# Transposing by DMA instead of by TensorE in an attention kernel followed by a feed-forward: q, k, tails and attention outputs

## Chip, cores, metric

The kernel runs on one core of a Trainium2 chip. The metric is the device time of one execution in microseconds. Before the change it was 450.04 us (median of 4 runs, 449.12 to 450.78). "Span" is the time of the profiled execution as its trace shows it, a little below the device time.

## The reference

Eight batches of eight heads of attention over 576 positions (head size 64) with a relative-position bias, then a bilinear feed-forward:

```python
scores = q @ k.T / 8 + bias[bucket(|i - j|), head]        # 8 x 8 x 576 x 576
attn   = exp(scores - max) / sum(...)
x      = (attn @ v) laid out as 4608 tokens x 512
out    = ((x @ w_a) * (x @ w_b)) @ w_out                   # w_a, w_b: 512 x 1536, w_out: 1536 x 512
```

## The kernel before

Work goes by pairs of heads: 32 pairs, four to a batch. 512 of the 576 positions are the main part; the other 64 are the tail. Pair `p` is worked on in step `p`. From step 4 on, each step also holds feed-forward units of four matmuls each (seven or eight in steps 4 to 8, nine in later ones), of a chunk of 512 tokens; chunk `c` is batch `c`'s main part and from chunk 1 on its units fill steps `4c+5` to `4c+8`. The kernel's matmuls take q and k with the head dimension on the partitions, and the attention output likewise, so all of them are transposed on TensorE into PSUM and copied to SBUF:

```python
def transposes(ps, src, p, tag):
    b, hp = divmod(p, 4)
    for t in range(NM):                                   # NM = 4 blocks of 128 x 128
        x = (st[p][tag][:, t, :, :] if early(b) else      # early: batches 0 and 1
             src[b % 2][:, 512 * t + 128 * hp:512 * t + 128 * hp + 128])
        nc.tensor.transpose(ps[:, 128 * t:128 * t + 128], x, ident[:, :])

def t_q(p, eng=None):
    ps = ps_tr.tile([128, 1024], BF16, tag="tr", name=f"trq{p}")
    transposes(ps, qn, p, "qr")
    nc.tensor.transpose(ps[:, SM:SM + 128], qkt[b % 2][:, 2 * hp:2 * hp + 2, :], ident[:, :])
    ...                                                   # one large copy and four of 64 x 64

def t_x(p, eng=None):                                     # attention output of pair p
    ps = ps_tr.tile([128, 1024], BF16, tag="tr", name=f"trx{p}")
    for jq in range(5):
        nc.tensor.transpose(ps[:, 128 * jq:128 * jq + 128], XG[p % 2][:, jq, :, :], ident[:, :])
    copy(eng, xn_sb[hp][:, SM * b:SM * b + SM], ps[:, 0:SM])
    copy(eng, xn_sb[hp][:, SM * B + ST * b:SM * B + ST * b + ST], ps[:, SM:S])

# one step s (cut, the lambdas left out): U is a place for feed-forward units
steps += [qk(s, 0), U, ex(s, 1), A(0, 1, 2), U, mul(s, 0), t_q(s + 1), U, mul(s, 1), qk(s, 2), ..., U,
          ex(s, 3), t_k(s + 1), U, mul(s, 2), A(3, 4), U, mul(s, 3), qk_tail(s), U, t_x(s - 1), U,
          mul_tail(s), U]
b = s // 4 + 1
if s > 4 and s % 4 == 1 and b < B:                        # loads of the next batch, on GpSimd's queue
    load_q(b, 0, 8); load_k(b, 0, 8); load_tails(b); load_v(b, 0, 8); load_vt(b)
```

A load stands in the program at some step, but in the traces below it starts when GpSimd has come to it, behind the loads before it, and the buffer that it overwrites has been read for the last time (a semaphore tells GpSimd so: at 207.26 us the q load goes out after 18.47 us of waiting for PE's `trq_3162`).

The softmax here doesn't subtract the row's maximum and nothing guards it: scores larger than these inputs give would overflow.

Of the kernel before, what the change touches and what calls it, by code (L numbers as in the profile page):

```python
# [13 lines left out]
def kernel(  # L14
# [11 lines left out]
    nc = tc.nc  # L26
    FP32 = mybir.dt.float32
    BF16 = mybir.dt.bfloat16
# [3 lines left out]
    B, H, S, Dh = 8, 8, 576, 64  # L32
    NB = 32
    NM = 4
    SM = 128 * NM
    ST = S - SM
# [6 lines left out]
    NP = B * H // 2  # L43
# [33 lines left out]
    ident = const.tile([128, 128], BF16, name="ident")  # L77
# [11 lines left out]
    qn = [wpool.tile([128, H * NM * Dh], BF16, name=f"qn{i}") for i in range(2)]  # L89
    kn = [wpool.tile([128, H * NM * Dh], BF16, name=f"kn{i}") for i in range(2)]  # L90
    vn = [wpool.tile([128, H * NM * Dh], BF16, name=f"vn{i}") for i in range(2)]
    qkt = [wpool.tile([128, H, Dh], BF16, name=f"qkt{i}") for i in range(2)]
    vm = [wpool.tile([128, H, NM, Dh + 1], BF16, name=f"vm{i}") for i in range(2)]
    vt = [wpool.tile([128, H // 2, 2, Dh + 1], BF16, name=f"vt{i}") for i in range(2)]

    QT = [wpool.tile([128, S + 2 * ST], BF16, name=f"QT{i}") for i in range(3)]
    KT = [wpool.tile([128, SM + 2 * ST], BF16, name=f"KT{i}") for i in range(3)]
    XG = [wpool.tile([128, 5, 2, Dh], BF16, name=f"XG{i}") for i in range(2)]

    NW = 3  # L100
# [9 lines left out]
    def early(b):  # L110
        return b < 2
# [24 lines left out]
    def load_v(b, h0, h1):  # L136
        load4(v, vn[b % 2], b, h0, h1)

    def load_tails(b):
        for src, o in ((q, 0), (k, 64)):  # L140
            nc.gpsimd.dma_start(out=qkt[b % 2][o:o + 64, :, :],
                                in_=src[b, :, SM:S, :].transpose([1, 0, 2]))

    def load_vt(b):
        for hh in range(2):
            nc.gpsimd.dma_start(  # L146
                out=vt[b % 2][64 * hh:64 * hh + 64, :, hh, 0:Dh],
                in_=v[b, hh:H:2, SM:S, :].transpose([1, 0, 2]))
# [15 lines left out]
    nc.sync.dma_start(out=oh_sb[0:NB, :], in_=oh_handle.ap())  # L164
    nc.scalar.dma_start(out=ident[:, :], in_=id_handle.ap())
    nc.vector.memset(zero_sb[:, :], 0.0)
    for i in range(2):
        nc.vector.memset(vt[i][0:64, :, 1, :], 0.0)
        nc.vector.memset(vt[i][64:128, :, 0, :], 0.0)
        nc.vector.memset(vt[i][0:64, :, 0, Dh:Dh + 1], 1.0)  # L170
        nc.vector.memset(vt[i][64:128, :, 1, Dh:Dh + 1], 1.0)
# [48 lines left out]
    for hp in range(H // 2):  # L220
# [3 lines left out]
        if hp == 0:  # L224
            for hh in range(2):
                nc.sync.dma_start(out=Wt_sb[64 * hh:64 * hh + 64, :, :],
                                  in_=bass.AP(tensor=tab, offset=hh * TB + 512,
                                              ap=[[1, 64], [2 * TB, H // 2], [1, 192]]))
    for i in range(3):
        nc.vector.memset(QT[i][0:64, S + ST:], 0.0)  # L230
        nc.vector.memset(QT[i][64:128, S:S + ST], 0.0)
        nc.vector.memset(KT[i][0:64, SM + ST:], 0.0)
        nc.vector.memset(KT[i][64:128, SM:SM + ST], 0.0)


    st = [dict() for _ in range(NP)]
# [1 line left out]
    def copy(eng, out, in_):  # L238
        if eng is nc.scalar:
            nc.scalar.activation(out=out, in_=in_, func=ACTF.Copy)  # L240
        else:
            nc.vector.tensor_copy(out=out, in_=in_)
# [11 lines left out]
                    "p (h t d) -> p t h d", h=2, t=NM))  # L254
            st[p][tag] = r

    def transposes(ps, src, p, tag):
        b, hp = divmod(p, 4)
        for t in range(NM):
            x = (st[p][tag][:, t, :, :] if early(b) else  # L260
                 src[b % 2][:, 512 * t + 128 * hp:512 * t + 128 * hp + 128])
            nc.tensor.transpose(ps[:, 128 * t:128 * t + 128], x, ident[:, :])

    def t_q(p, eng=None):
        b, hp = divmod(p, 4)
        ps = ps_tr.tile([128, 1024], BF16, tag="tr", name=f"trq{p}")
        transposes(ps, qn, p, "qr")
        nc.tensor.transpose(ps[:, SM:SM + 128], qkt[b % 2][:, 2 * hp:2 * hp + 2, :], ident[:, :])  # L268
        qT, kT = QT[p % 3], KT[p % 3]
        if early(b):  # L270
            copy(eng, qT[:, 0:SM].rearrange("d (p t) -> d p t", t=NM),
                 ps[:, 0:SM].rearrange("d (t p) -> d p t", t=NM))
            copy(eng, qT[:, SM:S], ps[:, SM:S])
        else:
            copy(eng, qT[:, 0:S], ps[:, 0:S])
        for hh in range(2):
            r = slice(64 * hh, 64 * hh + 64)
            nc.vector.tensor_copy(out=kT[r, SM + ST * hh:SM + ST * hh + ST], in_=ps[r, S:S + ST])
            nc.vector.tensor_copy(out=qT[r, S + ST * hh:S + ST * hh + ST], in_=ps[r, SM:S])

    def t_k(p, eng=None, pool=None, tag="tr"):
        b, hp = divmod(p, 4)
        ps = (pool or ps_tr).tile([128, 1024], BF16, tag=tag, name=f"trk{p}")
        transposes(ps, kn, p, "kr")
        copy(eng, KT[p % 3][:, 0:SM], ps[:, 0:SM])
        st[p]["at"] = [None] * NM

    def v_in(b, h0, h1):
        if b < 2:
# [4 lines left out]


    def qk(p, t0):
        qT, kT = QT[p % 3], KT[p % 3]
        for t in (t0, t0 + 1):
            ps = ps_sc.tile([128, 2, 512], FP32, tag="sc", name=f"qk{p}_{t}")
            for hh in range(2):  # L300
                r = slice(64 * hh, 64 * hh + 64)
                nc.tensor.matmul(out=ps[:, hh, :], lhsT=kT[r, 128 * t:128 * t + 128],  # L302
                                 rhs=qT[r, 0:SM], start=True, stop=True)
            st[p]["ps", t] = ps

    def ex(p, t):
# [9 lines left out]


    def qk_tail(p):
        hp = p % 4
        qT, kT = QT[p % 3], KT[p % 3]  # L320
        ps = ps_sc.tile([128, 2, 512], FP32, tag="sc", name=f"qkt{p}")
        for t in range(NM):
            nc.tensor.matmul(
                out=ps[:, 0, :].rearrange("p (h t c) -> p h t c", h=2, t=NM)[:, :, t, :],
                lhsT=kT[:, 128 * t:128 * t + 128], rhs=qT[:, S:S + 2 * ST],
                start=True, stop=True)
        nc.tensor.matmul(out=ps[:, 1, :], lhsT=kT[:, SM:SM + 2 * ST], rhs=qT[:, 0:SM],
                         start=True, stop=True)
        pt = ps_tr.tile([128, 512], FP32, tag="tr", name=f"qktt{p}")
        nc.tensor.matmul(out=pt[:, 0:ST], lhsT=kT[:, SM:SM + 2 * ST], rhs=qT[:, SM:S],  # L330
                         start=True, stop=True)
        st[p]["ps"] = (ps, pt)

    def ex_tail(p):
# [55 lines left out]

    def t_x(p, eng=None):
        b, hp = divmod(p, 4)
        ps = ps_tr.tile([128, 1024], BF16, tag="tr", name=f"trx{p}")
        for jq in range(5):
            nc.tensor.transpose(ps[:, 128 * jq:128 * jq + 128], XG[p % 2][:, jq, :, :], ident[:, :])  # L395
        copy(eng, xn_sb[hp][:, SM * b:SM * b + SM], ps[:, 0:SM])
        copy(eng, xn_sb[hp][:, SM * B + ST * b:SM * B + ST * b + ST], ps[:, SM:S])
        st[p].clear()
# [97 lines left out]
    for s in range(4, NP + 1):  # L496
        new = s < NP
        U = "unit"
        A = lambda *jq: (lambda: [av(s - 1, j) for j in jq])
        steps = []  # L500
        if new:
            steps += [lambda: (qk(s, 0), ex(s, 0))]
        if s == 4:
            steps += [A(0, 1, 2), lambda: ex(s, 1), lambda: t_q(s + 1), A(3, 4),
                      lambda: mul(s, 0), lambda: t_x(s - 1), U, lambda: mul(s, 1), U,
                      lambda: (qk(s, 2), ex(s, 2)), U, lambda: ex(s, 3), lambda: t_k(s + 1), U,
                      lambda: mul(s, 2), U, lambda: mul(s, 3), lambda: (qk_tail(s), ex_tail(s)),
                      U, U, lambda: mul_tail(s)]
        elif new:
            steps += [U, lambda: ex(s, 1), A(0, 1, 2), U, lambda: mul(s, 0)]  # L510
            if s + 1 < NP:
                steps += [lambda: t_q(s + 1)]
            steps += [U, lambda: mul(s, 1), lambda: (qk(s, 2), ex(s, 2)), U, lambda: ex(s, 3)]
            if s + 1 < NP:
                steps += [lambda: t_k(s + 1)]
            steps += [U, lambda: mul(s, 2), A(3, 4), U, lambda: mul(s, 3),
                      lambda: (qk_tail(s), ex_tail(s)), U, lambda: t_x(s - 1), U,
                      lambda: mul_tail(s), U]
        else:
            steps += [A(0, 1, 2), U, U, U, A(3, 4), U, U, U, lambda: t_x(s - 1), U, U, U]  # L520
        reorder(s + 1)
        b = s // 4 + 1
        if s > 4 and s % 4 == 1 and b < B:
            load_q(b, 0, 8)
            load_k(b, 0, 8)
            load_tails(b)
            load_v(b, 0, 8)
            load_vt(b)
        quota = quotas.get(s, 9)
        seen, put = 0, 0  # L530
        nu = sum(1 for x in steps if x is U)
        for x in steps:
            if x is U:
                seen += 1
                n = (quota * seen + nu - 1) // nu - put
                put_units(n)
                put += n
            else:
                x()
        if new:  # L540
            v_next(s)
# [31 lines left out]
```

## Time and profile before

| | before |
|---|---|
| device time | 450.04 us |
| span | 449.3 us |
| TensorE (PE) busy | 424.7 us, 95% |
| VectorE busy | 287.4 us, 64% |
| one steady step | 11.88 us |

From the profile's page: the span, the busy time of each engine, PE's busy tenths and granted clock (tenths of full speed) in 40 equal slices, and the chain of waits by engine.

```profile
span 449.3 us, 9012 instructions
PE 424.7 (95%) x3578; PEld 221.1 (49%) x3643; DVE 287.4 (64%) x838; ACT 245.8 (55%) x350; POOL 88.9 (20%) x117
PE   5676999999999999999999999999999999999995
PEclk8579999999999999999999999999999999999999
PE 83%; DVE 10%; DMA 3%; issue 2%; ACT 1%; SPq 0%; DVEq 0%; ACTq 0%
```

After the first four slices PE is never short of work and the clock is full: from 47 to 445 us PE is busy for 394.1 of 398.0 us at a granted clock of 1.00. What PE does is what the kernel costs. The timeline of PE in one step (start, duration, line, output<-input, count) shows what a transpose costs there:

```profile
189.54 0.44 PE L395 MATMUL trx_2895<-ident,XG_112 128*128 128x128 bf16 x5
189.82 0.38 PE L426 MATMUL po_3_2890<-wo,g_128 128*128 128x512 bf16 x1
...
192.84 0.38 PE L406 MATMUL pa_0_2939<-xn_123,wa_113 128*128 128x512 bf16 x1
```

The durations overlap: 128x512 matmuls are listed with 0.38 us each and start 0.21 to 0.22 us apart (188.68, 188.89, 189.11 us). The cost is the distance between starts: five transposes take 0.28 us, from 189.54 to 189.82. At 192.84 the fourth matmul of a new chunk reads `xn_123`, the output of the batch's last pair.

GpSimd's timeline at the same place, with the wait that ended before each issue in brackets:

```profile
187.55 1.23 POOL L146 DMA_DIRECT2D vt_104<-in_v_dram  x2 [17.29 <-PE av_3_2848 L376]
207.26 3.53 POOL L123 DMA_DIRECT2D qn_93<-in_q_dram  x4 [18.47 <-PE trq_3162 L268]
```

The q loads wait until PE has transposed the last of the old q, so they start at 207 us.

### The profile page before, as it was taken

How to read it: one execution, taken by the hardware profiler on the slowest of the kernel's cores; microseconds unless marked ns; L12 is line 12 of the kernel's file. 1: busy time of each engine (PE TensorE's matmuls, PEld its weight loads, DVE VectorE, ACT ScalarE, POOL GpSimd, SP SyncE). 2: the span in 40 equal slices, each digit the busy share in tenths (PEclk: the TensorE clock that was granted, in tenths of full speed). 3: DMA queues.
4: the chain of work that ended last, by engine and by line, in shares of the span. 5: the costliest groups of instructions: out<-in, count | busy, mean ns of one | idle time of the engine just before them, and what ended most of it. 6: DMA issues, size and time to landing. Idle time of an engine off the chain costs nothing.

```text
span 449.3 us, 9012 instructions
## 1 busy us (share of the span) xinstructions
PE 424.7 (95%) x3578; PEld 221.1 (49%) x3643; DVE 287.4 (64%) x838; ACT 245.8 (55%) x350; POOL 88.9 (20%) x117
## 2 busy tenths in 40 slices
PE   5676999999999999999999999999999999999995
PEld 2264455555555555555555555555555554444442
DVE  5579789668766787577856786587658862330320
ACT  2678566556655665566556665566556652322321
POOL 9456365010801070105200350100000000000000
PEclk8579999999999999999999999999999999999999
DMA  9999999420942097207912290200010002002004
GB/s 101 219 200 203 192 148 76 82 65 1 107 72 63 15 84 72 77 25 49 104 49 54 16 137 27 76 1 1 23 71 2 1 1 94 1 0 93 1 1 94
DMA packets 87370, 30.35 MB, mean 68 GB/s; under 512 B 64760, under 2 KB 82712, under 8 KB 87328
## 3 DMA queue, kind: packets, MB, share of 16 engines
q0 software_dynamic: 80144, 18.88, 45.0%
q1 hardware_dynamic: 6992, 10.86, 7.3%
q8 instruction: 28, 0.46, 0.4%
q14 instruction: 14, 0.11, 0.1%
q10 hardware_dynamic: 192, 0.03, 0.0%
HBM read 39.18 MB, written 9.45 MB: 108 GB/s over the span
## 4 chain that ended last, share of the span: by engine, by line
PE 83%; DVE 10%; DMA 3%; issue 2%; ACT 1%; SPq 0%; DVEq 0%; ACTq 0%
DMA Wt<-bias_tab 2%; DVE XG_111 L387 1%; DVE g_125 L419 1%; DVE g_124 L419 1%; PE warm L208 1%; PE po_1_1335 L426 1%; PE po_0_1275 L426 1%; DMA bias_tab<-tab_sb 1%; PE po_1_2057 L426 1%; PE po_1_4869 L426 1%; PE po_1_3463 L426 1%; PE po_1_2760 L426 1%; PE po_1_4166 L426 1%; PE po_2_1403 L426 1%; PE po_3_6071 L426 1%
## 5 line engine op out<-in xcount | busy, mean ns | idle before, releaser
L416 PEld LDWEIGHTS <-wb_118 128*128 128x128 bf16 x144 | 12.4, 97 | 16.6 <-issue 5.6
L406 PEld LDWEIGHTS <-wa_114 128*128 128x128 bf16 x144 | 12.5, 98 | 15.3 <-issue 3.4
L416 PEld LDWEIGHTS <-wb_117 128*128 128x128 bf16 x144 | 12.4, 97 | 14.9 <-issue 4.7
L406 PEld LDWEIGHTS <-wa_113 128*128 128x128 bf16 x144 | 12.5, 98 | 14.6 <-issue 3.0
L416 PEld LDWEIGHTS <-wb_116 128*128 128x128 bf16 x144 | 12.3, 97 | 14.9 <-issue 5.1
L406 PEld LDWEIGHTS <-wa_115 128*128 128x128 bf16 x144 | 12.7, 98 | 13.4 <-issue 2.5
L123 POOL DMA_DIRECT2D qn_93<-in_q_dram x12 | 11.0, 925 | 38.6 <-PE trq_3162 L268 18.5
L123 POOL DMA_DIRECT2D qn_94<-in_q_dram x12 | 10.6, 886 | 40.2 <-PE trq_2459 L268 18.5
L146 POOL DMA_DIRECT2D vt_104<-in_v_dram x8 | 4.9, 620 | 53.7 <-PE av_3_2848 L376 17.3
L132 POOL DMA_DIRECT2D kn_95<-in_k_dram x12 | 10.6, 906 | 6.8 <-DVE qr_844 L251 6.6
L146 POOL DMA_DIRECT2D vt_103<-in_v_dram x8 | 5.0, 640 | 34.8 <-PE av_3_2145 L376 17.3
L132 POOL DMA_DIRECT2D kn_96<-in_k_dram x12 | 10.6, 912 | 0.0
L395 PEld LDWEIGHTS <-XG_112 128*128 128x128 bf16 x80 | 5.8, 98 | 5.4 <-DVE XG_112 L387 1.5
L395 PEld LDWEIGHTS <-XG_111 128*128 128x128 bf16 x80 | 5.8, 98 | 5.1 <-DVE XG_111 L387 1.8
L302 PEld LDWEIGHTS <-KT_108 64*128 64x128 bf16 x88 | 2.8, 95 | 10.7 <-issue 8.6
L419 DVE TENSOR_TENSOR g_124<-pb_0_5871,ha_0_5869 128x512 bf16<-128x512 f32 x1 | 0.7, 692 | 11.4 <-PE pb_0_5871 L416 11.4
L302 PEld LDWEIGHTS <-KT_109 64*128 64x128 bf16 x88 | 2.6, 95 | 10.4 <-issue 10.4
L426 PEld LDWEIGHTS <-g_124 128*128 128x128 bf16 x36 | 3.5, 97 | 7.0 <-issue 4.7
L302 PEld LDWEIGHTS <-KT_110 64*128 64x128 bf16 x80 | 2.4, 95 | 8.2 <-issue 8.1
L114 POOL DMA_DIRECT2D vn_98<-in_v_dram x5 | 4.2, 836 | 7.4 <-DVE vm_102 L291 6.8
L426 PEld LDWEIGHTS <-g_126 128*128 128x128 bf16 x36 | 3.5, 98 | 4.3
L426 PEld LDWEIGHTS <-g_134 128*128 128x128 bf16 x36 | 3.5, 98 | 4.3
(3194 smaller groups left out, 1643.6 us busy)
## 6 DMA issues: line engine op xcount, KB each, us to landing
qn_93<-in_q_dram POOLq DMA_DIRECT2D x16, 128.0 KB, 4.2
kn_95<-in_k_dram POOLq DMA_DIRECT2D x16, 128.0 KB, 5.1
qn_94<-in_q_dram POOLq DMA_DIRECT2D x16, 128.0 KB, 5.4
kn_96<-in_k_dram POOLq DMA_DIRECT2D x16, 128.0 KB, 4.9
wo<-in_moe_w_out_dram POOLq DMA_DIRECT2D x1, 1536.0 KB, 16.4
vn_97<-in_v_dram POOLq DMA_DIRECT2D x3, 512.0 KB, 7.1
vn_98<-in_v_dram POOLq DMA_DIRECT2D x3, 512.0 KB, 5.8
vn_97<-in_v_dram POOLq DMA_DIRECT2D x2, 256.0 KB, 10.7
```

The source lines that it names most:

```text
L114: nc.gpsimd.dma_start(out=dst[:, 256 * h0:256 * h1].rearrange("p (h x) -> p h x", x=256), in_=src[b, h0:h1, 0:SM, :].rearrange("h (p t) d ...
L123: nc.gpsimd.dma_start(out=qn[b % 2][:, :].rearrange("p (t h d) -> p t h d", h=H, t=NM)[:, t, h0:h1, :], in_=q[b, h0:h1, 128 * t:128 * t + ...
L132: nc.gpsimd.dma_start(out=kn[b % 2][:, :].rearrange("p (t h d) -> p t h d", h=H, t=NM)[:, t, h0:h1, :], in_=k[b, h0:h1, t:SM:NM, :].transp ...
L146: nc.gpsimd.dma_start(out=vt[b % 2][64 * hh:64 * hh + 64, :, hh, 0:Dh], in_=v[b, hh:H:2, SM:S, :].transpose([1, 0, 2]))
L208: nc.tensor.matmul(out=warm[:, :], lhsT=zero_sb[:, 0:128], rhs=zero_sb[:, :], start=True, stop=True)
L302: nc.tensor.matmul(out=ps[:, hh, :], lhsT=kT[r, 128 * t:128 * t + 128], rhs=qT[r, 0:SM], start=True, stop=True)
L387: nc.vector.tensor_tensor(out=xg[0:np_, j0:j0 + n, :, :], in0=pav[0:np_, s0:s0 + n, :, 0:Dh], in1=rc.unsqueeze(3).to_broadcast([np_, n, 2, ...
L395: nc.tensor.transpose(ps[:, 128 * jq:128 * jq + 128], XG[p % 2][:, jq, :, :], ident[:, :])
L406: nc.tensor.matmul(out=pa[:, :], lhsT=wa_sb[df // 4][:, mc, 128 * (df % 4):128 * (df % 4) + 128], rhs=xn_sb[mc][:, 512 * c:512 * c + 512], ...
L416: nc.tensor.matmul(out=pb[:, :], lhsT=wb_sb[df // 4][:, mc, 128 * (df % 4):128 * (df % 4) + 128], rhs=xn_sb[mc][:, 512 * c:512 * c + 512], ...
L419: nc.vector.tensor_tensor(out=g_sb[df][:, :], in0=pb[:, :], in1=ff["ha"][:, :], op=MULT)
L426: nc.tensor.matmul(out=po[:, :], lhsT=g_sb[df][:, 128 * tt:128 * tt + 128], rhs=wo_sb[:, df, :], start=(df == 0), stop=(df == NDF - 1))
```

## The change

The intent is to take the transposes off the engine that sets the time, and their copies off VectorE. For batches 2 to 7, K, Q and the tails of a whole batch are transposed by three DMAs from SBUF to SBUF, one step ahead of the batch. The outputs of pairs 4 to 30 are transposed by DMA straight into the feed-forward's input. All transposing DMAs are issued by SP, whose queue also stores the output. The loads of the next batch move one step up in the program. The core of the diff (the operand tiles and the early batches' path are cut, lines are joined and the comments added):

```diff
+    def t_batch(b):
+        i = b % 2
+        for dst, src in ((KB, kn), (QB, qn)):                       # 512 KB each
+            nc.sync.dma_start_transpose(
+                out=dst[i][:, :, :, :].rearrange("d t h c -> d (t h) c"), in_=src[i][:, :])
+        nc.sync.dma_start_transpose(                                 # tails, 256 KB
+            out=ZB[i][:, :, :, :].rearrange("d h i c -> d (h i) c"),
+            in_=tl[i][:, :, :, :].rearrange("p h i x -> p (h i x)"))
 ...
     def t_x(p, eng=None):
         b, hp = divmod(p, 4)
+        if 4 <= p < NP - 1:
+            nc.sync.dma_start_transpose(
+                out=xn_sb[hp][:, SM * b:SM * b + SM].rearrange("d (j c) -> d j c", j=4),
+                in_=XG[p % 2][:, 0:4, :, :].rearrange("p j h d -> p (j h d)"))
+            c0 = SM * B + ST * b
+            nc.sync.dma_start_transpose(out=xn_sb[hp][:, c0:c0 + ST],
+                in_=XG[p % 2][0:ST, 4, :, :].rearrange("p h d -> p (h d)"))
+            st[p].clear()
+            return
 ...
-        if s > 4 and s % 4 == 1 and b < B:
+        if s % 4 == 3 and b < B:
+            t_batch(b)
+        if s % 4 == 0 and b < B:
             load_q(b, 0, 8)
             load_k(b, 0, 8)
             load_tails(b)
             load_v(b, 0, 8)
+        if s % 4 == 1 and 1 < b < B:
             load_vt(b)
```

More of the change, by code (lines that the diff above doesn't have):

```diff
@@ L91 @@
     vn = [wpool.tile([128, H * NM * Dh], BF16, name=f"vn{i}") for i in range(2)]
-    qkt = [wpool.tile([128, H, Dh], BF16, name=f"qkt{i}") for i in range(2)]
+    tl = [wpool.tile([128, H // 2, 2, 128], BF16, name=f"tl{i}") for i in range(2)]
     vm = [wpool.tile([128, H, NM, Dh + 1], BF16, name=f"vm{i}") for i in range(2)]
     vt = [wpool.tile([128, H // 2, 2, Dh + 1], BF16, name=f"vt{i}") for i in range(2)]
-    QT = [wpool.tile([128, S + 2 * ST], BF16, name=f"QT{i}") for i in range(3)]
-    KT = [wpool.tile([128, SM + 2 * ST], BF16, name=f"KT{i}") for i in range(3)]
+    QT = [wpool.tile([128, NM, 128], BF16, name=f"QT{i}") for i in range(2)]
+    KT = [wpool.tile([128, NM, 128], BF16, name=f"KT{i}") for i in range(2)]
+    ZT = [wpool.tile([128, 2, 128], BF16, name=f"ZT{i}") for i in range(2)]
+    QB = [wpool.tile([128, NM, H // 2, 128], BF16, name=f"QB{i}") for i in range(2)]
+    KB = [wpool.tile([128, NM, H // 2, 128], BF16, name=f"KB{i}") for i in range(2)]
+    ZB = [wpool.tile([128, H // 2, 2, 128], BF16, name=f"ZB{i}") for i in range(2)]
     XG = [wpool.tile([128, 5, 2, Dh], BF16, name=f"XG{i}") for i in range(2)]
@@ L139, in load_tails @@
     def load_tails(b):
-        for src, o in ((q, 0), (k, 64)):
-            nc.gpsimd.dma_start(out=qkt[b % 2][o:o + 64, :, :],
-                                in_=src[b, :, SM:S, :].transpose([1, 0, 2]))
+        for i, src in enumerate((q, k)):
+            for hh in range(2):
+                nc.gpsimd.dma_start(
+                    out=tl[b % 2][64 * hh:64 * hh + 64, :, i, Dh * hh:Dh * hh + Dh],
+                    in_=src[b, hh:H:2, SM:S, :].transpose([1, 0, 2]))
     def load_vt(b):
@@ L166 @@
     nc.vector.memset(zero_sb[:, :], 0.0)
+    for i in range(2):
+        nc.vector.memset(tl[i][0:64, :, :, Dh:], 0.0)
+        nc.vector.memset(tl[i][64:128, :, :, 0:Dh], 0.0)
     for i in range(2):
@@ L228 @@
                                               ap=[[1, 64], [2 * TB, H // 2], [1, 192]]))
-    for i in range(3):
-        nc.vector.memset(QT[i][0:64, S + ST:], 0.0)
-        nc.vector.memset(QT[i][64:128, S:S + ST], 0.0)
-        nc.vector.memset(KT[i][0:64, SM + ST:], 0.0)
-        nc.vector.memset(KT[i][64:128, SM:SM + ST], 0.0)
     st = [dict() for _ in range(NP)]
@@ L255, in reorder, with transposes @@
             st[p][tag] = r
-    def transposes(ps, src, p, tag):
-        b, hp = divmod(p, 4)
+    def transposes(ps, p, tag):
         for t in range(NM):
-            x = (st[p][tag][:, t, :, :] if early(b) else
-                 src[b % 2][:, 512 * t + 128 * hp:512 * t + 128 * hp + 128])
-            nc.tensor.transpose(ps[:, 128 * t:128 * t + 128], x, ident[:, :])
+            nc.tensor.transpose(ps[:, 128 * t:128 * t + 128], st[p][tag][:, t, :, :], ident[:, :])
     def t_q(p, eng=None):
@@ L265, in t_q @@
         b, hp = divmod(p, 4)
+        if p >= NP or not early(b):
+            return
         ps = ps_tr.tile([128, 1024], BF16, tag="tr", name=f"trq{p}")
-        transposes(ps, qn, p, "qr")
-        nc.tensor.transpose(ps[:, SM:SM + 128], qkt[b % 2][:, 2 * hp:2 * hp + 2, :], ident[:, :])
-        qT, kT = QT[p % 3], KT[p % 3]
-        if early(b):
-            copy(eng, qT[:, 0:SM].rearrange("d (p t) -> d p t", t=NM),
-                 ps[:, 0:SM].rearrange("d (t p) -> d p t", t=NM))
-            copy(eng, qT[:, SM:S], ps[:, SM:S])
-        else:
-            copy(eng, qT[:, 0:S], ps[:, 0:S])
@@ L276, in t_q @@
-        for hh in range(2):
-            r = slice(64 * hh, 64 * hh + 64)
-            nc.vector.tensor_copy(out=kT[r, SM + ST * hh:SM + ST * hh + ST], in_=ps[r, S:S + ST])
-            nc.vector.tensor_copy(out=qT[r, S + ST * hh:S + ST * hh + ST], in_=ps[r, SM:S])
+        transposes(ps, p, "qr")
+        copy(eng, QT[p % 2][:, :, :].rearrange("d a c -> d (a c)").rearrange("d (p t) -> d p t", t=NM),
+             ps[:, 0:SM].rearrange("d (t p) -> d p t", t=NM))
     def t_k(p, eng=None, pool=None, tag="tr"):
@@ L282, in t_k @@
         b, hp = divmod(p, 4)
+        if p >= NP or not early(b):
+            return
         ps = (pool or ps_tr).tile([128, 1024], BF16, tag=tag, name=f"trk{p}")
-        transposes(ps, kn, p, "kr")
-        copy(eng, KT[p % 3][:, 0:SM], ps[:, 0:SM])
-        st[p]["at"] = [None] * NM
+        transposes(ps, p, "kr")
+        for i in range(2):
+            nc.tensor.transpose(ps[:, SM + 128 * i:SM + 128 * i + 128], tl[b % 2][:, hp, i, :],
+                                ident[:, :])
+        copy(eng, KT[p % 2][:, :, :], ps[:, 0:SM].rearrange("d (t c) -> d t c", t=NM))
@@ new lines, in t_k, with operands @@
+        copy(eng, ZT[p % 2][:, :, :], ps[:, SM:SM + 256].rearrange("d (i c) -> d i c", i=2))
+    def t_batch(b):
[6 more added lines that the diff above has]
+            in_=tl[i][:, :, :, :].rearrange("p h i x -> p (h i x)"))
+    def operands(p):
+        b, hp = divmod(p, 4)
+        if early(b):
+            return QT[p % 2][:, :, :], KT[p % 2][:, :, :], ZT[p % 2][:, :, :]
+        return QB[b % 2][:, :, hp, :], KB[b % 2][:, :, hp, :], ZB[b % 2][:, hp, :, :]
@@ L296, in qk @@
     def qk(p, t0):
-        qT, kT = QT[p % 3], KT[p % 3]
+        qT, kT, _ = operands(p)
+        st[p].setdefault("at", [None] * NM)
         for t in (t0, t0 + 1):
@@ L301, in qk @@
                 r = slice(64 * hh, 64 * hh + 64)
-                nc.tensor.matmul(out=ps[:, hh, :], lhsT=kT[r, 128 * t:128 * t + 128],
-                                 rhs=qT[r, 0:SM], start=True, stop=True)
+                nc.tensor.matmul(out=ps[:, hh, :], lhsT=kT[r, t, :], rhs=qT[r, :, :],
+                                 start=True, stop=True)
             st[p]["ps", t] = ps
@@ L318, in qk_tail @@
     def qk_tail(p):
-        hp = p % 4
-        qT, kT = QT[p % 3], KT[p % 3]
+        qT, kT, z = operands(p)
         ps = ps_sc.tile([128, 2, 512], FP32, tag="sc", name=f"qkt{p}")
@@ L324, in qk_tail @@
                 out=ps[:, 0, :].rearrange("p (h t c) -> p h t c", h=2, t=NM)[:, :, t, :],
-                lhsT=kT[:, 128 * t:128 * t + 128], rhs=qT[:, S:S + 2 * ST],
-                start=True, stop=True)
-        nc.tensor.matmul(out=ps[:, 1, :], lhsT=kT[:, SM:SM + 2 * ST], rhs=qT[:, 0:SM],
-                         start=True, stop=True)
+                lhsT=kT[:, t, :], rhs=z[:, 0, :], start=True, stop=True)
+        nc.tensor.matmul(out=ps[:, 1, :], lhsT=z[:, 1, :], rhs=qT, start=True, stop=True)
         pt = ps_tr.tile([128, 512], FP32, tag="tr", name=f"qktt{p}")
-        nc.tensor.matmul(out=pt[:, 0:ST], lhsT=kT[:, SM:SM + 2 * ST], rhs=qT[:, SM:S],
-                         start=True, stop=True)
+        for hh in range(2):
+            nc.tensor.matmul(out=pt[:, 0:ST], lhsT=z[:, 1, :], rhs=z[:, 0, ST * hh:ST * hh + ST],
+                             start=(hh == 0), stop=(hh == 1))
         st[p]["ps"] = (ps, pt)
@@ L392, in t_x @@
         b, hp = divmod(p, 4)
+        if 4 <= p < NP - 1:
[3 more added lines that the diff above has]
+            c0 = SM * B + ST * b
+            nc.sync.dma_start_transpose(
+                out=xn_sb[hp][:, c0:c0 + ST],
+                in_=XG[p % 2][0:ST, 4, :, :].rearrange("p h d -> p (h d)"))
+            st[p].clear()
+            return
         ps = ps_tr.tile([128, 1024], BF16, tag="tr", name=f"trx{p}")
```

## The prediction

> **What bounds the kernel now.** The instruction table gives TensorE 424.7 us busy (95% of 449.3), VectorE 64%, ScalarE 55%; the chain of waits is 83% PE. Start-up takes 47 us (the chain runs over the 9.1 us bias-table DMA and VectorE); then, to 367 us, feed-forward and attention interleave with PE busy 99%; then 82 us of feed-forward alone. In the timeline one steady step (a head pair plus nine feed-forward units) lasts 11.88 us with no PE gap. A microsecond taken from PE's stream there is a microsecond of time; one taken from VectorE is nothing.
>
> **Removed from PE.** 311 of about 3640 weight-load/matmul pairs (order of instructions): nine q/k/tail transposes for pairs 8 to 31, five output transposes for pairs 4 to 30, less one extra tail transpose per early pair and one extra 64-column matmul per pair. In the timeline five transposes take 0.28 us of PE's stream, so 0.055 us each[...]. 311 x 0.055 = 17 us, all on the critical path. A late step falls from 11.88 to 11.1 us.
>
> **Removed from VectorE.** About 2 us of copies per late pair, some 45 us, off the path except early.
>
> **Added.** (1) Four memsets of the tail tiles (about 0.37 us pitch, from the existing memsets) stand ahead of the bias-table arithmetic on the start-up chain: +1.4 us; two more tail loads per batch on POOL: up to +1 us. Fewer small copies in early steps give back 1 to 2 us. Net 0 to +1 us.
> (2) Per batch two 512 KB transposes and one of 256 KB, started about one step (11 to 12 us) before the first score matmul needs K and Q. [...] Just hidden: 0 to 1 us lost in each of six batches.
> (3) The output transpose of a batch's last pair now gates the next chunk's fourth feed-forward matmul. The output store ahead of it issues at 189.1 us; that matmul starts at 192.8, or 192.5 without the PE transposes. So about 3.1 us are free, the next loads start just then[...]: 0 to 2 us lost at each of six boundaries, say 5 us.
>
> **Sum.** 450.1 - 17 + 0.5 (start) + 2 (K, Q) + 5 (boundaries) - 4 (copies that held PE at 45 to 60 us) = 436.6; I take 436 us, range 428 to 456. Chances: faster 0.62, same 0.23, slower 0.15.
>
> **What would show each step.** PE busy about 17 us lower; VectorE busy near 243 us; steps of 11.1 us inside a batch; waits of the first score matmuls of a batch (on DMA KB or QB) under 1 us; waits of a chunk's first feed-forward matmuls on DMA xn, 0 to 2 us, six of them; table DMA 1.4 us later. [...]
>
> **What would make it wrong.** Transposing DMAs slower[...]: if a 512 KB one takes over 6 us, each microsecond more costs 2 us per batch, 12 in all; at 10 us each the kernel is slower than before. SP issues transposes and output stores in order[...]. Load packets would lengthen the boundaries. If all is hidden: 429 to 431.

The sum came to 436.6 us, taken as 436.

## The result

The changed kernel is correct and takes 473.51 us (median of 4 runs, 472.41 to 475.42). The ratio to before is 1.0527, with a 95% interval of 1.0483 to 1.0571: slower by 5.3%. Ratios here are the mean time of one kernel's fast runs over that of the other's of the same rounds, so they differ a little from the ratio of the medians. The forecast was 436 us, faster by 3%.

The page of the changed kernel, the same lines:

```profile
span 470.6 us, 8393 instructions
PE 417.7 (89%) x3274; PEld 206.9 (44%) x3332; DVE 243.5 (52%) x597; ACT 246.8 (52%) x353; POOL 97.9 (21%) x133
PE   7566999799977996979959799799999999999995
PEclk9999999999998999889989899899999999999998
PE 68%; DMA 19%; DVE 1%; issue 1%; SPq 0%; ACT 0%; POOL 0%; DVEq 0%; ACTq 0%
```

The work did go away: 311 fewer weight loads (PEld 3643 to 3332), 304 fewer PE matmul records (a few records can be missing from a trace) and 44 us less VectorE time. But PE now has holes between slices 8 and 26, its clock dips in many of the same slices, and DMA holds 19% of the chain. The list of PE's waits (who, for what, us in total, times, longest) names the holes:

```profile
PE qk_0_3175 L318 <- DMA QB_112<-qn_94: 4.6, 1, 4.6
PE qk_0_2555 L318 <- DMA QB_111<-qn_93: 3.7, 1, 3.7
PE qk_0_1935 L318 <- DMA QB_112<-qn_94: 3.3, 1, 3.3
PE qk_0_3795 L318 <- DMA QB_111<-qn_93: 3.3, 1, 3.3
PE pa_0_2089 L430 <- DMA xn_129<-XG_118: 3.2, 1, 3.2
PE pa_0_3329 L430 <- DMA xn_129<-XG_118: 3.2, 1, 3.2
PE pa_0_2709 L430 <- DMA xn_129<-XG_118: 2.7, 1, 2.7
PE qk_0_1324 L318 <- DMA QB_111<-qn_93: 2.7, 1, 2.7
...
PE pa_0_1469 L430 <- DMA qn_93<-in_q_dram: 1.0, 1, 1.0
```

Five batches (2 to 6) wait for the transposed Q, 17.6 us in all. Four chunks (1 to 4) wait at their start for the last pair's output, 10.1 us in all; the line naming a load is one of them: that matmul reads no load, and the list put its wait down to a transfer that landed at the same moment. Batch 7 and chunks 5 and 6 do not wait.

SP's timeline (start, time to issue) for batch 5 and, after the dots, for batch 7:

```profile
227.66 1.96 SPq L291 DMA_TRANSPOSE KB_114<-kn_96  x1
229.84 8.37 SPq L291 DMA_TRANSPOSE QB_112<-qn_94  x1
...
336.54 2.56 SPq L291 DMA_TRANSPOSE QB_112<-qn_94  x1
```

The same instruction takes SP 8.37 us to issue in batch 5 and 2.56 us in batch 7. The view of one tile gives the times from the start of the issue to landing; for `QB_112` (batches 3, 5 and 7):

```profile
L291 SPq DMA_TRANSPOSE QB_112<-qn_94 x3: 2565/8274/8370, 122.1 to 336.5; - x3
DMA to landing us min/median/max: 5.7/12.5/13.6
```

The quick one is batch 7's, which has no batch after it to load; the slow ones are batches 3 and 5, and batch 4's Q took 13.0 us. (Batch 6's landing is not in the trace.) GpSimd's timeline shows what stands beside the others:

```profile
197.00 1.23 POOL L153 DMA_DIRECT2D vt_104<-in_v_dram  x2 [21.25 <-PE av_3_2634 L390]
198.22 3.62 POOL L128 DMA_DIRECT2D qn_93<-in_q_dram  x4
...
229.30 0.90 POOL L119 DMA_DIRECT2D vn_97<-in_v_dram  x1 [21.48 <-DVE vm_101 L306]
```

Here lies what the diff did not show. The q and k buffers are now free long before, because a DMA has read them, so GpSimd no longer waits for PE's q transposes. It stops at the small `vt` load, and when that is released at the end of the batch's last attention work, `vt`, q, k and tails all go at once: at 197 us, where the last pair's output transpose (198.96 us) and the chunk boundary (201.4 us) are. The view of that transpose alone (`--tile xn_129 --window 198.9:199.1`) gives its landing:

```profile
DMA to landing us min/median/max: 5.9/5.9/5.9
```

The v load then waits for VectorE to read the old v, at the end of the step before the batch transposes, and so starts at 229.30 us, between the K and the Q transpose.

Last, PE around one wait:

```profile
243.55 0.61 PE L318 MATMUL qk_0_3175<-QB_112,KB_114 64*128 64x512 bf16 x2 [4.56 <-DMA QB_112<-qn_94]
...
245.35 0.63 PE L450 MATMUL po_1_3183<-wo,g_132 128*128 128x512 bf16 x1
245.77 0.63 PE L450 MATMUL po_1_3183<-wo,g_133 128*128 128x512 bf16 x1
...
249.49 0.38 PE L450 MATMUL po_1_3183<-wo,g_138 128*128 128x512 bf16 x1
249.70 0.38 PE L450 MATMUL po_1_3183<-wo,g_139 128*128 128x512 bf16 x1
```

After the wait, matmuls follow one another at 0.42 us (245.35 to 245.77) in place of 0.21 us (249.49 to 249.70), up to 249 us. The busy time by stretch gives the granted clock (here the number after the engines' columns): 0.57 in both stretches after the wait, 1.00 later.

```profile
242.00:246.00 4.00, 2.12 (x7) 0.75 (x9) 0.00 (x0) 1.80 (x2) 0.00 (x0) 0.57 0.67 165
246.00:250.00 4.00, 4.00 (x35) 2.53 (x34) 1.87 (x4) 0.14 (x1) 0.00 (x0) 0.57 0.00 0
250.00:254.00 4.00, 3.95 (x35) 1.86 (x35) 1.19 (x5) 2.43 (x3) 0.45 (x1) 1.00 0.18 70
```

Between the start-up and the last 5 us the changed kernel has half clock (granted 0.50) in seven stretches of 3.41 us, two of them in a row (242.55 to 249.37 us). They follow six of the nine waits; those of batches 2 and 3 and of chunk 1 were paid only once. In these 23.9 us PE was busy for 21.3, so an estimate of their cost is half of that, 10.6 us. An experiment below tests the cause.

**Theory.** Four things: (a) the transpose of Q is slowed by the v load beside it (Q is issued at 229.84 us, the v load at 229.30); (b) K and Q are issued late, since SP issues in program order and reaches them only behind the outputs of the step before (`xn_127` at 224.97 and 226.26 us, K at 227.66); (c) the last output transpose (198.96 us) is slowed by the loads that the change moved onto the chunk boundary (197.00 to 206.50 us); (d) most of the waits (six of nine) cost again by the halved clock. The rivals: two 512 KB transposes in a row are slow by themselves; an output transpose is too slow for the boundary by itself; the clock falls for another reason. Where expectations say that transfers share the DMA engines, that is theory: the runs show landing times, not what is shared.

### The profile page after: what moved, and what is told of

It is laid out like the page before. It is cut to its first block, busy times and chain, and to the rows that moved or that the text cites. A ratio compares the mean times of both kernels' runs of the same rounds, so it can differ in the third digit from the quotient of the medians.

```text
span 470.6 us, 8393 instructions
## 1 busy us (share of the span) xinstructions
PE 417.7 (89%) x3274; PEld 206.9 (44%) x3332; DVE 243.5 (52%) x597; ACT 246.8 (52%) x353; POOL 97.9 (21%) x133
## 4 chain that ended last, share of the span: by engine, by line
PE 68%; DMA 19%; DVE 1%; issue 1%; SPq 0%; ACT 0%; POOL 0%; DVEq 0%; ACTq 0%
DMA QB_111<-qn_93 7%; DMA QB_112<-qn_94 6%; DMA xn_129<-XG_118 4%; DMA tl_100<-in_k_dram 1%; DMA qn_93<-in_q_dram 1%; PE po_1_3183 L450 1%; PE po_1_3803 L450 1%; PE po_1_2563 L450 1%; PE po_2_1372 L450 1%; PE po_3_5541 L450 1%; PE po_0_5270 L450 1%; PE po_0_4381 L450 1%; PE po_3_4524 L450 1%; PE po_2_5524 L450 1%; PE po_1_5507 L450 1%
## 5 line engine op out<-in xcount | busy, mean ns | idle before, releaser
L430 PEld LDWEIGHTS <-wa_119 128*128 128x128 bf16 x144 | 13.4, 100 | 17.8 <-issue 4.9
L430 PEld LDWEIGHTS <-wa_121 128*128 128x128 bf16 x144 | 13.4, 98 | 17.4 <-issue 2.5
L440 PEld LDWEIGHTS <-wb_122 128*128 128x128 bf16 x144 | 13.0, 101 | 17.2 <-issue 6.9
L440 PEld LDWEIGHTS <-wb_123 128*128 128x128 bf16 x144 | 12.9, 97 | 17.2 <-issue 4.7
L440 PEld LDWEIGHTS <-wb_124 128*128 128x128 bf16 x144 | 12.5, 97 | 17.6 <-issue 7.2
L430 PEld LDWEIGHTS <-wa_120 128*128 128x128 bf16 x144 | 12.4, 97 | 16.1 <-issue 5.0
L153 POOL DMA_DIRECT2D vt_104<-in_v_dram x8 | 5.0, 627 | 59.5 <-PE av_3_2634 L390 21.2
L153 POOL DMA_DIRECT2D vt_103<-in_v_dram x8 | 5.0, 633 | 42.7 <-PE av_3_3254 L390 23.4
L119 POOL DMA_DIRECT2D vn_98<-in_v_dram x5 | 4.2, 837 | 44.0 <-DVE vm_102 L306 44.0
L119 POOL DMA_DIRECT2D vn_97<-in_v_dram x5 | 4.3, 865 | 39.4 <-DVE vm_101 L306 38.9
L137 POOL DMA_DIRECT2D kn_95<-in_k_dram x12 | 10.6, 906 | 7.3 <-DMA wo<-in_moe_w_out_dram 7.0
L318 PEld LDWEIGHTS <-KB_113 64*128 64x128 bf16 x96 | 2.9, 94 | 19.9 <-issue 19.9
L128 POOL DMA_DIRECT2D qn_93<-in_q_dram x12 | 10.9, 921 | 2.8 <-DVE QT_106 L247 1.4
L318 PEld LDWEIGHTS <-KB_114 64*128 64x128 bf16 x96 | 2.8, 95 | 18.5 <-issue 18.5
L128 POOL DMA_DIRECT2D qn_94<-in_q_dram x12 | 10.8, 909 | 0.6 <-DVE kr_1009 L256 0.4
L137 POOL DMA_DIRECT2D kn_96<-in_k_dram x12 | 10.6, 906 | 0.2 <-issue 0.2
L443 DVE TENSOR_TENSOR g_130<-pb_0_5341,ha_0_5339 128x512 bf16<-128x512 f32 x1 | 0.7, 692 | 11.4 <-PE pb_0_5341 L440 11.4
L450 PEld LDWEIGHTS <-g_130 128*128 128x128 bf16 x36 | 3.5, 98 | 6.4 <-issue 5.5
L147 POOL DMA_DIRECT2D tl_100<-in_q_dram x8 | 5.1, 651 | 3.7 <-DMA vn_97<-in_v_dram 3.5
L218 PE MATMUL warm<-zero_sb 128*128 128x512 bf16 x10 | 4.6, 626 | 1.2 <-DVE zero_sb L173 1.2
L450 PEld LDWEIGHTS <-g_132 128*128 128x128 bf16 x36 | 3.6, 101 | 4.6 <-issue 0.6
L450 PEld LDWEIGHTS <-g_136 128*128 128x128 bf16 x36 | 3.6, 101 | 4.6 <-issue 0.6
## 6 DMA issues: line engine op xcount, KB each, us to landing
vn_97<-in_v_dram POOLq DMA_DIRECT2D x3, 512.0 KB, 11.6
vn_98<-in_v_dram POOLq DMA_DIRECT2D x3, 512.0 KB, 11.6
vn_97<-in_v_dram POOLq DMA_DIRECT2D x2, 256.0 KB, 10.1
```

The costliest lines, as they stand in the source:

```text
L119: nc.gpsimd.dma_start(out=dst[:, 256 * h0:256 * h1].rearrange("p (h x) -> p h x", x=256), in_=src[b, h0:h1, 0:SM, :].rearrange("h (p t) d ...
L128: nc.gpsimd.dma_start(out=qn[b % 2][:, :].rearrange("p (t h d) -> p t h d", h=H, t=NM)[:, t, h0:h1, :], in_=q[b, h0:h1, 128 * t:128 * t + ...
L137: nc.gpsimd.dma_start(out=kn[b % 2][:, :].rearrange("p (t h d) -> p t h d", h=H, t=NM)[:, t, h0:h1, :], in_=k[b, h0:h1, t:SM:NM, :].transp ...
L147: nc.gpsimd.dma_start(out=tl[b % 2][64 * hh:64 * hh + 64, :, i, Dh * hh:Dh * hh + Dh], in_=src[b, hh:H:2, SM:S, :].transpose([1, 0, 2]))
L153: nc.gpsimd.dma_start(out=vt[b % 2][64 * hh:64 * hh + 64, :, hh, 0:Dh], in_=v[b, hh:H:2, SM:S, :].transpose([1, 0, 2]))
L218: nc.tensor.matmul(out=warm[:, :], lhsT=zero_sb[:, 0:128], rhs=zero_sb[:, :], start=True, stop=True)
```

## The experiments

Eight kernels ran, each with three timed rounds beside the kernel before, all correct. Steps are measured from one step's first exponential to the next one's in ScalarE's timeline.

### A third buffer for v

```diff
-    vn = [... for i in range(2)]
+    vn = [... for i in range(3)]        # and vn[b % 3] where it was vn[b % 2]
```

> The changed kernel with a third buffer for the v loads, so that a v load no longer waits for VectorE and no longer starts in the step of the K and Q transposes. Theory A (the slow Q transposes share the DMA engines with the v load): Q transposes land 5.5 to 7 us after issue in every batch (12.5 to 13.6 now, 5.7 in batch 7, which has no v load beside it), PE waits on QB fall from 17.6 us to under 3, the half-clock stretches after them go (5.8 us), time 452 to 457 us. Theory B (the second of two 512 KB transposes on one queue is slow by itself): landing stays 12 to 13 us, waits stay 15 to 18 us, time 471 to 475.

Measured: 451.3 us (one of its four runs was slow; the median of the others is 450.52), just under the range, ratio of fast runs 1.0002 (0.9958 to 1.0046). From the tile view of Q, over the batches that have a landing record (five of six):

```profile
DMA to landing us min/median/max: 5.6/5.9/6.4
```

The waits on QB are 2.5 us, once, in batch 2, where a v load still starts beside the K transpose (74.98 and 75.58 us). Theory (a) holds, in that the v load is what slows Q, and its rival falls: with the v load out of the step, the second transpose in a row lands as fast as the first. The waits at the boundaries (9.4 us on xn, and one of 1.0) stayed.

### The batch transposes one step earlier

```diff
-        if s % 4 == 3 and b < B:
+        if (s == 7 or (s > 7 and s % 4 == 2)) and b < B:
             t_batch(b)
```

> The changed kernel with the batch transposes put one step (11.3 us) earlier from batch 3 on, ahead of the v load. Both theories: waits on QB nearly gone from batch 3 on (2.7 us of batch 2 stays), time 452 to 458 us. Theory A: Q lands within 5.5 to 7 us; theory B: 12 to 13 us, but hidden.

Measured: 451.81 us (one of its four runs was slow; the median of the others is 451.38), ratio of fast runs 1.0015 (0.9973 to 1.0056), just under the range. Q lands 4.3 to 5.4 us after issue from batch 3 on; the only wait on QB left is batch 2's 2.7 us. Ahead of the v load the transposes are quick, as (a) says.

### No output by DMA

```diff
-        if 4 <= p < NP - 1:
+        if False:
```

> The changed kernel with all output transposes back on PE; q, k and tails still by DMA. PE gets 27 x 0.28 = 7.6 us back; the waits on xn (10.1 us) and the half-clock stretches after them (about 5.2 us) go; the waits on QB (17.6 us) and their half clock (5.8 us) stay. Time 464 to 468 us. Rival (the output transposes in the SP queue also delay the K and Q transposes): waits on QB fall to 10 us or less and the time to 458 or less.

Measured: 440.3 us, ratio 0.9786 (0.9758 to 0.9813). This was a miss of our expectation, and the rival written beside it is right: no wait on QB is left at all. SP's timeline for batch 3, first of this kernel:

```profile
97.41 4.81 SPq L291 DMA_TRANSPOSE KB<-kn  x1
102.39 6.86 SPq L291 DMA_TRANSPOSE QB<-qn  x1
```

and then of the changed kernel:

```profile
118.77 1.18 SPq L412 DMA_TRANSPOSE xn_127<-XG_118  x1
120.13 1.78 SPq L291 DMA_TRANSPOSE KB_114<-kn_96  x1
122.08 8.27 SPq L291 DMA_TRANSPOSE QB_112<-qn_94  x1
```

With no output transposes ahead of it in SP's queue, the K transpose starts two steps sooner. It then runs beside the q and k loads and lands after 13.5 us, Q after 12.2: slow, but hidden. So (b) is a cause of its own: slow transposes do harm only because they start late, and they start late because SP issues in order behind outputs that wait for VectorE (K at 97.41 us here, at 120.13 in the changed kernel, where SP had waited 8.3 to 10.4 us for VectorE ahead of each batch's `xn_127`). This kernel is already 2.1% faster than the one before (the interval lies on both sides of 2%, so by the rule of 2% its verdict is unclear), with 0.47 us less in each steady step.

### The outputs by DMA alone

The kernel before with only the `t_x` part of the diff; loads as before.

> The kernel before with only the output transposes of pairs 4 to 30 by DMA; q, k, tails and all loads as before. There the q and k loads start a step and more after a chunk boundary. Theory A (the last output transpose is slow in the changed kernel because the loads now start at the same moment): it lands in 2.4 to 2.8 us, PE waits on xn under 1 us in all, time 442 to 444 us. Rival (the transpose is too slow for the boundary by itself): waits of 1 to 3 us at each of six boundaries, time 450 to 460.

Measured: 445.34 us, ratio 0.9889 (0.986 to 0.9918), a little above the range that was set down. PE at a chunk boundary:

```profile
190.15 1.04 PE L416 MATMUL pa<-xn,wa 128*128 128x512 bf16 x4
```

Four matmuls in one row means no wait between them; the list of PE's waits has none on xn. In this kernel GpSimd's q loads start at 205 us, and the last output transposes of a batch land in 2.5 to 2.9 us where the trace records it. So the rival of (c) falls: the transpose is quick enough for the boundary. The gain was 0.2 us a step in place of the 0.28 us that five transposes cost, and one step early on ran partly at half clock (step 4 lasted 14.08 us in place of 12.65); where the rest of the 0.28 us goes was not found.

### The loads held until the output has landed

```diff
         if s % 4 == 1 and 1 < b < B:
+            nc.gpsimd.tensor_copy(out=gate_sb[0:1, 0:1],
+                                  in_=xn_sb[3][0:1, SM * (b - 2):SM * (b - 2) + 1])
             load_vt(b)
```

GpSimd copies one element that the last output transpose of a batch writes, so it reaches the loads only when that has landed (the copy at 148.46 us, after 22.19 us of waiting for the transpose, the first load at 148.97). (The tile for the element is left out here, and the line is broken.)

> The changed kernel with one tiny GpSimd copy of a value that the last output transpose of a batch writes, ahead of the loads that now start at a chunk boundary: the loads start only when that transpose has landed. Theory A (the last output transpose is slowed by the loads beside it): it lands in 2.4 to 2.9 us after issue in every batch (4.8 to 6.4 now), PE waits on xn fall from 10.1 us to under 1.5, half clock after them goes, time 456 to 460; waits on QB stay near 17 us. Rival (the transpose is too slow for the boundary by itself): waits of 1 us and more stay at most boundaries, time 463 or more.

Measured: 445.71 us, ratio 0.9896 (0.985 to 0.9942), below the range. The transpose that landed after 5.9 us in the changed kernel is here (192.98 us):

```profile
DMA to landing us min/median/max: 2.4/2.4/2.4
```

The last output of a batch lands in 2.4 us wherever the trace records it (five of six), and no wait on xn is left. That settles (c) from the other side. What neither theory said: the waits on QB fell too, from 17.6 to 9.2 us. Q still took 9.6 to 11.6 us where the v load stood beside it, against 12.5 to 13.6, though the v load started as close to it as before. Two things can be read from the traces. In batches 3 to 5 SP issued Q in 2.0 to 3.6 us here, against 8.3 to 8.8, and it was still slow: so it can land late without a long issue. And in each of the batches 3 to 6 of the changed kernel, with both transfers under way, the DMA nearly stopped: the windows view has stretches of 2 us with 8 to 11 GB/s (9 from 235 to 237 us). Here, in batches 3 to 5, the lowest such stretch that was found has 73. So running beside the load is not all of it; what made the DMA stop stays open.

### TensorE kept busy while it waits

```diff
+        if s % 4 == 0 and 12 <= s <= 24:
+            fill = ps_ff.tile([128, 512], FP32, tag="ffn", name=f"fill{s}")
+            for _ in range(14):
+                nc.tensor.matmul(out=fill[:, :], lhsT=zero_sb[:, 0:128], rhs=zero_sb[:, :],
+                                 start=True, stop=True)
```

> The changed kernel with 14 matmuls on zeros (3.0 us at full clock) just ahead of the first score matmul of batches 3 to 6, where PE waits 3.3 to 4.6 us for QB. If the half-clock stretches after these waits come from PE having been idle, they go and the time falls by about 5.8 us, to 466 to 469; waits of up to 1.6 us stay. If the clock falls for another reason (transposing DMAs beside, or the amount of work), the time stays at 472 to 475.

Measured: 464.47 us, ratio 1.0312 (1.0286 to 1.0338): 9 us faster than the changed kernel, by work that is of no use. PE at batch 5:

```profile
239.07 3.18 PE L552 MATMUL fill<-zero_sb 128*128 128x512 bf16 x14
242.19 0.60 PE L318 MATMUL qk<-QB,KB 64*128 64x512 bf16 x4
242.73 1.04 PE L450 MATMUL po<-wo,g 128*128 128x512 bf16 x4
```

The four matmuls after the score matmuls take 1.04 us from first start to last end, full clock, and steps 12, 16, 20 and 24 have none at half clock; in the changed kernel steps 16, 20 and 24 had. So (d) holds: idleness lowered the clock. The gain is larger than foretold because only 0.4 us of waiting was left in these four batches and not the 2.9 us that 14.9 less 4 x 3.0 leaves: Q landed sooner in this run too (8.9 to 12.7 us).

### Both cures together

The batch transposes at `s % 4 == 2` for every batch, and the loads held as above. Every transpose of the change stays on DMA.

> Both cures at once, all transposes still by DMA: batch transposes one step earlier (batch 2 too) and loads held until the boundary's output transpose has landed. If late start, shared DMA engines and half clock are the whole cause, no wait on QB or xn over 1 us is left, steps last 11.1 to 11.3 us throughout, and the time is 432 to 436 us, below before by 3 to 4%. If something else costs time too, it stays above 440.

Measured: 435.28 us (434.57 to 435.96), ratio 0.9663 (0.9639 to 0.9687): 3.4% faster than before. Its page:

```profile
span 432.8 us, 8398 instructions
PE 406.2 (94%) x3274; PEld 201.6 (47%) x3332; DVE 243.0 (56%) x597; ACT 246.2 (57%) x353; POOL 98.5 (23%) x139
PE   6476899999999999999999999999999999999995
PEclk8589999999999999999999999999999999999999
PE 87%; DVE 1%; issue 1%; ACT 0%; ACTq 0%; DVEq 0%
```

The holes, the dips of the clock and DMA's share of the chain are gone. Steps 9 to 30 last 11.11 to 11.29 us.

### Earlier, and the last output of a batch on TensorE

The same, but instead of holding the loads, `t_x` uses the DMA only where `hp < 3`.

> The same with the other cure of the boundary: the last pair's output of each batch transposed on PE again (6 x 0.28 us more PE work) and no hold on the loads. 434 to 438 us; no wait on QB or xn over 1 us. Rival (loads and transposes together still disturb PE): above 440.

Measured: 437.25 us, ratio 0.971 (0.9681 to 0.974), no wait on QB or xn. Six output transposes on PE cost 0.28 us each, 1.7 us; the difference to the version above is 2.0 us.

## Why the prediction was wrong

The sum of the changed kernel's span, every term measured but the rest, which is what is left over (the estimate from its half-clock stretches was 10.6):

| | us |
|---|---|
| span before | 449.3 |
| PE and VectorE work removed, start-up included (span of the cured version less span before) | -16.5 |
| five waits for Q | +17.6 |
| four waits for the last output | +10.1 |
| rest: matmuls at half clock after the waits (470.6 less the four terms above) | +10.1 |
| span of the changed kernel | 470.6 |

- **PE work removed: right in count, a little large in time.** The prediction said 17 us from 311 transposes at 0.055 us, a late step falling by 0.78 us to 11.1. The weight loads fell by just 311. In the cured version (both cures together) steps 9 to 30 last 11.20 us in the mean in place of 11.87: 0.67 us less, 14.7 us over these 22 steps. Its PE is busy 18.5 us less in all.
- **Copies that held PE at 45 to 60 us: this term failed too.** "- 4" was taken off for them. In that stretch PE's waits for VectorE are 1.3 us in the kernel before and in the cured version: there were no 4 us to win, and what there was did not go. So the terms -17, +0.5 and -4, -20.5 in sum, measured -16.5. The prediction's figure for everything hidden was 429 to 431 us; the cured version has everything hidden and takes 435.28. That this lies so near the forecast of 436, which counted 7 us of waits, is luck.
- **VectorE: right.** 243 us foretold, 243.5 measured.
- **Start-up: right.** The table DMA was issued 1.2 us later (6.31 against 5.14 us), and fewer copies gave it back: step 4 began at 42.4 us in place of 42.9.
- **Batch transposes: the step that failed.** The prediction put it as "Just hidden: 0 to 1 us lost in each of six batches". With no load beside them K and Q took 4.1 to 6.2 us each. Beside the v load Q took 12.5 to 13.6 us in batches 3 to 5, and both had landed only 14.5 to 15.8 us after K's issue; five batches lost 2.7 to 4.6 us. The term "+ 2 (K, Q)" measured 17.6. The prediction read the lead of one step rightly (11.3 to 11.4 us from K's issue to the wait in batches 3 to 6, 9.2 in batch 2), but took no load to stand beside these transposes. Its list of what would make it wrong named slow ones, but as a trait of every transposing DMA; K, issued just ahead of the v load, still landed in 5.0 and 5.1 us in batches 3 and 4. Q took 5.6 to 6.4 us with a third v buffer, 12.5 to 13.6 beside the load.
- **Boundaries: right in kind, too small in part.** "0 to 2 us lost at each of six boundaries, say 5 us" became 1.0, 3.2, 2.7 and 3.2 us at four and nothing at two: the term "+ 5 (boundaries)" measured 10.1. The transpose alone takes 2.4 us; with the loads, which the change itself moved there, 4.8 to 6.4 us. The prediction named the loads but put no cost of their own on them.
- **The clock: missing.** Nothing in the prediction allowed for a slower clock after a wait. It was 10 us of the 38 us by which the changed kernel exceeds its cured version (470.6 less 432.8).

What remains open: what stopped the DMA while Q's transpose and the v load were both under way, why that was absent in the run with held loads and in batch 5 of the run with useless matmuls (where Q took 8.9 us), and where 0.08 us a step went of the outputs' gain when they alone were moved.

## What to carry to other kernels

When a change frees a buffer earlier, ask what the next transfer into it will now run beside: a load starts where its semaphores let it, not where it stands in the program (in the kernel before GpSimd waited 18.47 us for PE ahead of the q load at 207.26 us; in the changed kernel that load followed `vt` at once, at 198.22 us). Before a DMA takes over work that was hidden on an in-order engine, check three things in the trace: what stands ahead of it in the issuing queue, which loads are under way in its window (Q landed after 12.5 to 13.6 us beside the v load), and how long the consumer would idle. Waits of 1 to 4.6 us on TensorE cost a third as much again at the halved clock here (10.1 us on 27.7), so a small loss at many places can outweigh a large saving, and moving an issue by one step and holding the loads for 5 us (from 180.8, when PE had read the old v tail, to 185.8 us in the cured version) turned 5% slower into 3% faster.

## What the runs measured that an estimate can start from

- A 128x128 transpose on TensorE in a busy stream cost 0.055 us (five in 0.28 us).
- A 128x512 transpose by DMA took 2.4 us from issue to landing with no load beside it.
- SP was held for 1.2 us by the last 128x512 transposing DMA of a batch, for 1.7 to 3.9 us by a 128x2048 one with no load beside it (the third v buffer, batches 3 to 7), and for up to 8.8 us with one.
- A transposing DMA of 512 KB took 4.1 to 6.2 us with no load beside it. Beside one 512 KB load from GpSimd's queue it took 12.5 to 13.6 us in the changed kernel and 8.9 to 12.7 in two other runs; in the changed kernel that load took about 12 us, against 5.7 to 7.2 in the run with the third v buffer (batch 4 on).
- A wait of 2.66 us was followed by half clock in the changed kernel (chunk 3); one of 3.3 us there (batch 3) and one of 3.27 us with the third v buffer (chunk 4) were not. So the length of the wait alone did not decide it here, and what did is not shown. For the wait of 2.66 us (stretch, us, PE busy, ..., granted clock third from the end):

```profile
201.63:205.04 3.41, 0.75 (x4) 0.27 (x3) 0.00 (x0) 0.88 (x1) 3.41 (x5) 1.00 2.61 148
205.04:208.45 3.41, 3.19 (x31) 2.25 (x31) 0.75 (x2) 1.51 (x2) 2.78 (x5) 0.50 2.09 191
```
